# Query and key rows kept in DRAM once per part and doubled by the loads

## The chip, the cores and the metric

One core of a Trainium2 chip runs one transformer block. The metric is the device time of one launch in microseconds; the core has a matrix engine (TensorE, PE below; PEld is its weight load), VectorE (DVE), ScalarE (ACT), GpSimd (POOL) and SyncE (SP), and here SP issues every DMA.

## The reference

What is computed, cut to what matters (batch 1, S = 2048 rows, D = 512, 32 heads of 16):

```python
mod = (silu(c) @ w_mod).reshape(1, 6, 1, D)         # sa, ca, ga, sb, cb, gb
h = layernorm(x) * (1 + ca) + sa
q, k, v = split(h @ wqkv)                           # each [32, S, 16]
p = softmax(q @ k.T * 16 ** -0.5)
x = x + ga * ((p @ v).reshape(S, D) @ wo)
h = layernorm(x) * (1 + cb) + sb
x = x + gb * (mish(h @ w1 + b1) @ w2)               # w1: [512, 1792]
```

## The kernel before, in words

**Products of two parts.** A float32 value is kept as two parts, hi (rounded to the format in which PE multiplies) and lo (the rest). A product of two such values is taken as hi·hi + hi·lo + lo·hi. For a score of one head this is one matmul over 64 rows of a Q tile and a K tile: 3 x 16 = 48 rows hold the three combinations, row 48 and 49 of the Q tile hold the negated running maximum in two parts (mt) against rows of ones in K, and the other rows are zeros. Two heads share a tile, one at partitions 0 to 63 and one at 64 to 127 (`s` in the code).

**Where the rows lie.** A projection unit (`qk_unit`, one of Q or K, one of four column blocks `ct` of 8 heads, one of four blocks `tb` of 512 sequence rows) leaves a bank of 128 x 512 in PSUM. Its `fin` makes qh and ql of it, and `put` stores them to DRAM: to `qscr` for Q (50 rows for each head: hi, hi, lo of the first of the 16 values, hi, hi, lo of the second, and so on, then two rows of zeros) and to `kscr` for K (48 rows: hi, lo, hi of each value). For Q these are three DMAs, qh being stored twice; for K two, one of them with qh twice. A pair of heads `pp` is brought back by `load_q` (one DMA for each head, 50 x 512 values) and `load_k` (one for each head, 48 x 2048) into tiles `qa` and `ka`, of which there are five each, used in turn.

**The stages.** In the prologue (up to about 52 us) the layer norm, the first Q and K projections and part of V are made; for each `tb` the K block of the first 8 heads is stored and then loaded into the tiles of the first two pairs (`load_k(pp, tb)`, 48 x 512 for each head), while `load_q(pp, 48)` loads their Q. After this `constants` writes zeros, and copies of ones (line L1318) fill the K tiles 2 to 4. Then come steps `t`, two half steps `h` each. From t = -20 on a step makes maximum tiles (L471 on PE, reduced on DVE at L473) and the projections that are left (L126), from t = 0 on also scores (L507, with the exponential on ACT at L515), the product with V (L535) and, between them, the remaining projections and the MLP of earlier rows (L132). Sixteen steps are a group of four heads (two pairs) and 512 Q rows; there are 32 groups.

**What sets the order.** The program is written in the order in which each engine is to work. Work for SP hangs on half steps (`at(h, ...)`): the maximum rows of group n go out at half step 32n - 5 (`put` in `max_rows`, L496, four small DMAs into rows 48 and 49 of the `qa` tiles), the group's second pair is loaded five half steps after the rows of the group before, and the first pair earlier. SP takes its DMAs strictly in order: one that waits holds back all behind it. The DMAs share eight completion semaphores in turn, so a DMA also waits for the one issued eight before it. In the kernel's tail no Q or K load is left.

**Tiles with few buffers.** qh and ql have two buffers each, so the third unit's copies wait until the first unit's stores have landed. The weights of the next projection (`slice_load`, wr, L214) have one buffer; ACT and POOL split them into wh and wl (L91, L98) before the next units run. Projections use two banks in turn.

Of the kernel before, what the change touches and what calls it, by code (L numbers as in the profile page):

```python
# [8 lines left out]
F32 = mybir.dt.float32  # L9
# [9 lines left out]
def adaln_block(ctx: ExitStack, tc: tile.TileContext, x, wqkv, wo, w1, b1, w2, c, w_mod, out):  # L19
    nc = tc.nc  # L20
    P = 128
    S, D = x.shape[1], x.shape[2]
    F = w1.shape[1]
    H = 32
    DH = D // H
    DK = D // P
    FT = F // P
    TB = 512
# [23 lines left out]
    dram = ctx.enter_context(tc.tile_pool(name="dram", bufs=1, space=DRAM))  # L52
    ps = ctx.enter_context(tc.tile_pool(name="ps", bufs=1, space=PSUM))

    kscr = dram.tile([H, 48, S], F32, name="kscr")
    qscr = dram.tile([H, 50, S], F32, name="qscr")
    vscr = dram.tile([G, P, VROW], F32, name="vscr")
    woscr = dram.tile([DK, P, 2, D], F32, name="woscr")
    w1scr = dram.tile([FT, P, 2, D], F32, name="w1scr")
# [26 lines left out]
    def dap(t, off, ap):  # L86
        return bass.AP(tensor=t.tensor, offset=t.offset + off, ap=ap)

    def hi_copy(eng, hi, src):
        if eng == "a":  # L90
            nc.scalar.copy(hi, src)  # L91
        elif eng == "v":
            nc.vector.tensor_copy(hi, src)
        else:
            nc.gpsimd.tensor_scalar(hi, src, 1.0, 0.0, op0=ALU.mult, op1=ALU.add)

    def lo_sub(eng, lo, src, hi):
        (nc.gpsimd if eng == "p" else nc.vector).tensor_sub(lo, src, hi.bitcast(F32))  # L98
# [12 lines left out]
    def mm3(acc, ah, al, bh, bl, late="a"):  # L111

        n = len(ah)
        seq = ((ah, bh), (ah, bl), (al, bh)) if late == "a" else ((ah, bh), (al, bh), (ah, bl))
        seq = [(l[k], r[k]) for l, r in seq for k in range(n)]
        for i, (l, r) in enumerate(seq):
            mm(acc, l, r, i == 0, i == len(seq) - 1)
# [20 lines left out]
    def pe_run():  # L138
        while pe_queue:
            mm_go(pe_queue.pop(0))  # L140
# [13 lines left out]
    def bank(tag="ms"):  # L154
        return ring() if tag == "ring" else ps.tile([P, TB], F32, tag=tag, name="bk", bufs=1)
# [25 lines left out]
    def clear(h):  # L181

        return h if h < 60 or h % 32 < 25 else h - h % 32 + 34

    def at(h, f):

        hooks.setdefault(h, []).append(f)
# [29 lines left out]
    def slice_split(kind, i, pool=None, eng="p"):  # L217
        raw = slices[kind, i]
        w = raw.shape[2]
        hi = (pool or qp).tile([P, DK, w], F32R, tag="wh", name="wh", bufs=2)  # L220
        lo = (pool or qp).tile([P, DK, w], F32R, tag="wl", name="wl", bufs=2)
        hi_copy("a", hi, raw)
        lo_sub(eng, lo, raw, hi)
        slices[kind, i] = (hi, lo)

    def qk_unit(kind, ct, tb, tag):

        wh, wl = slices[kind, ct]
        acc = bank(tag)
        ts_ = slice(tb * TB, (tb + 1) * TB)  # L230
        mm3(acc, [wh[:, k, :] for k in range(DK)], [wl[:, k, :] for k in range(DK)],
            [h_h[:, k, ts_] for k in range(DK)], [h_l[:, k, ts_] for k in range(DK)], "b")

        def fin(h=None):
            qh = qp.tile([P, TB], F32R, tag="qh", name="qh", bufs=2)
            ql = qp.tile([P, TB], F32R, tag="ql", name="ql", bufs=2)
            if h is None:
                hi_copy("a", qh, acc)
                lo_sub("v", ql, acc, qh)
            else:  # L240
                qf = ql.bitcast(F32)
                nc.scalar.copy(qf, acc)
                hi_copy("p", qh, qf)
                lo_sub("p", ql, qf, qh)
            scr, rows = (qscr, 50) if kind == 0 else (kscr, 48)

            def put():
                put_away.add((kind, ct, tb))
                o = 8 * ct * rows * S + tb * TB
                if kind == 0:  # L250
                    for r, src in ((2, ql), (0, qh), (1, qh)) if h else ((0, qh), (1, qh), (2, ql)):
                        nc.sync.dma_start(dap(scr, o + r * S, [[rows * S, 8], [3 * S, DH], [1, TB]]), src.bitcast(F32))
                    return
                hi = qh.bitcast(F32)
                twice = bass.AP(tensor=hi.tensor, offset=hi.offset, ap=[list(hi.ap)[0], [0, 2], [1, TB]])
                both = (dap(scr, o, [[3 * S, P], [2 * S, 2], [1, TB]]), twice),                     (dap(scr, o + S, [[3 * S, P], [1, TB]]), ql.bitcast(F32))
                for to, src in reversed(both) if h else both:
                    nc.sync.dma_start(to, src)

            put() if h is None else at(clear(h + (5 if h > 60 else 2)), put)  # L260
        return fin
# [22 lines left out]
                put() if h is None else at(h + 1, put)  # L284
        return fin

    def load_q(pp, rows=50):
        n, j = divmod(pp, 2)
        qb, g = divmod(n, G)
        h = 4 * g + 2 * j  # L290
        qt = qa[pp % NR].bitcast(F32)
        assert (0, h // 8, qb) in put_away, (pp, put_away)
        for s in range(2):
            nc.sync.dma_start(qt[64 * s:64 * s + rows, :], qscr[h + s, :rows, qb * TB:(qb + 1) * TB])

    def load_k(pp, tb=None):
        n, j = divmod(pp, 2)
        h = 4 * (n % G) + 2 * j
        kt = ka[pp % NR].bitcast(F32)
        at_ = slice(0, S) if tb is None else slice(tb * TB, (tb + 1) * TB)  # L300
        assert {(1, h // 8, i) for i in (range(NB) if tb is None else (tb,))} <= put_away, (pp, put_away)
        for s in range(2):
            nc.sync.dma_start(kt[64 * s:64 * s + 48, at_], kscr[h + s, :, at_])

    def load_pair(pp):
        load_q(pp)
        load_k(pp)


    with ExitStack() as es:  # L310
# [23 lines left out]
        zer = lp.tile([P, TB], F32, name="zer")  # L334
# [12 lines left out]
        def stats_tb(tb):  # L347

            mv = lp.tile([P, 4, 2], F32, tag="ln_mv4", name="ln_mv4", bufs=2)
            rs = rss[tb] = lp.tile([P, 4, 4], F32, tag="ln_rs4", name="ln_rs4", bufs=3)  # L350
            for i in range(4):
                st_ = lp.tile([P, 6], F32, tag="ln_st", name="ln_st", bufs=4)
                nc.vector.bn_stats(out=st_, in_=xts[4 * tb + i])
                nc.vector.bn_aggr(out=mv[:, i, :], in_=st_)
            nc.gpsimd.tensor_scalar(rs[:, 0, :], mv[:, :, 1], 1.0, EPS, op0=ALU.mult, op1=ALU.add)
            nc.gpsimd.tensor_scalar(rs[:, 3, :], mv[:, :, 0], -1.0, 0.0, op0=ALU.mult, op1=ALU.add)
            nc.gpsimd.tensor_tensor(rs[:, 1, :], rs[:, 0, :], nhalf.to_broadcast([P, 4]), op=ALU.pow)
            nc.gpsimd.tensor_mul(rs[:, 2, :], rs[:, 3, :], rs[:, 1, :])
# [38 lines left out]
        def zeros(i):  # L397
            for b in (48, 112):
                nc.sync.dma_start(qa[i][b:b + 16, :].bitcast(F32), zer[:16, :])
# [6 lines left out]
        def constants():  # L406
            for i in range(2, NR):
                zeros(i)
            for q4 in range(S // TB):
                nc.sync.dma_start(dap(qscr, 48 * S + q4 * TB, [[50 * S, H], [S, 2], [1, TB]]), zer[:64, :])  # L410
            nc.sync.dma_start(dap(vscr, VROW - 16, [[VROW, P], [P * VROW, G], [1, 16]]), zer[:, :16 * G])
            nc.sync.dma_start(b1c, b1.rearrange("(f p) -> p f", p=P))

        def unit(fin):
            pe_run()
            fin()

        for tb in range(NB):
            if tb + 2 < NB:
                stats_tb(tb + 2)  # L420
            if tb == 0:
                slice_split(2, 0, eng="v")
            parts = []
            for kind in (1, 0) if tb == 0 else (1,):
                fin = qk_unit(kind, 0, tb, "ring")
                parts.append((pe_queue[2 * DK:], fin))
                del pe_queue[2 * DK:]
                pe_run()
            if tb in (1, 2):
                for kc in (2 * tb - 2, 2 * tb - 1):  # L430
                    unit(v_unit(0, kc, "ring"))
            if tb + 1 < NB:
                tr_tb(tb + 1, CUT1)
            for late, fin in parts:
                pe_queue.extend(late)
                unit(fin)
            if tb + 1 < NB:
                tr_tb(tb + 1, CUT2)
            if tb + 2 < NB:
                apply_tb(tb + 2)  # L440
            if tb == 0:
                for pp in range(2):
                    load_q(pp, 48)
            for pp in range(2):
                load_k(pp, tb)
        constants()
        slice_split(1, 1)

# [3 lines left out]
    ap = ctx.enter_context(tc.tile_pool(name="ap", bufs=1, reuse_waits="tile"))  # L452
# [909 lines left out]
```

## Time and profile before

| | us |
|---|---|
| median of three runs | 1707.33 (1706.47 to 1710.11) |
| the profiled execution's own time | 1705.91 |
| its span, first to last instruction | 1704.1 |
| PE busy in the span | 1667.8 |
| DVE busy | 1427.7 |
| ACT busy | 1342.4 |
| mean share of the 16 DMA engines, q1 | 48.9% |
| HBM written | 51.44 MB |

PE works in all but about 36 us of the span. In the rows below, a timeline row has start, length, engine, line, operation, out<-in and, in brackets, how long the engine stood idle before it and what ended that; SPq is the issue of a DMA, and its length is the time on the queue, not the transfer's. A row of the waits has the sum, the number and the longest of the waits. A row of windows has the stretch, its length, then the busy time of PE, PEld, DVE, ACT and POOL with instruction counts, the granted PE clock, the DMA share and GB/s. A row of a tile's view has shortest, median and longest duration in ns.

### The profile page before, as it was taken

The numbers are of one execution on the slowest core, as the hardware profiler recorded it, in microseconds if no ns is written. First come the engines' busy times: TensorE is split into PE (matmuls) and PEld (weight loads), VectorE is DVE, ScalarE is ACT, GpSimd is POOL, SyncE is SP. The second block draws the span as 40 slices with busy tenths as digits, with TensorE's granted clock in tenths as the row PEclk, the third lists the DMA queues.
The fourth block names the chain that finished last, engine by engine and source line by source line (L and its number), as shares of the span: only waits on it lengthen the run. The fifth ranks groups of instructions, "written<-read, shape, count | busy, mean of one in ns | idle before, by whom it ended". The sixth has DMA issues, their size and how long they took to land.

```text
span 1704.1 us, 32797 instructions
## 1 busy us (share of the span) xinstructions
PE 1667.8 (98%) x12236; PEld 929.6 (55%) x12236; DVE 1427.7 (84%) x2352; ACT 1342.4 (79%) x2605; POOL 889.5 (52%) x868
## 2 busy tenths in 40 slices
PE   7999999999999999999999999999999999999998
PEld 5755665555435455555555555555555555554677
DVE  6888898888898888888888888888888888881467
ACT  6247777777778898888889898888888888889364
POOL 5155215565503288755524397654534597646642
PEclk9999999999999999999999999999999999999999
DMA  7677567776772342435343644334442635332362
GB/s 242 186 223 214 128 160 211 245 233 212 237 207 58 109 128 73 126 80 148 90 127 74 189 109 96 101 108 125 114 102 73 174 99 130 93 106 82 124 225 72
DMA packets 113992, 240.03 MB, mean 141 GB/s; under 512 B 24048, under 2 KB 49648, under 8 KB 107784
## 3 DMA queue, kind: packets, MB, share of 16 engines
q1 hardware_dynamic: 113832, 237.92, 48.9%
q8 instruction: 97, 1.59, 0.4%
q14 instruction: 63, 0.52, 0.1%
HBM read 179.95 MB, written 51.44 MB: 136 GB/s over the span
## 4 chain that ended last, share of the span: by engine, by line
PE 85%; POOL 6%; ACT 3%; DMA 3%; DVE 1%; issue 1%; SPq 1%; DVEq 0%; ACTq 0%; POOLq 0%
PE bk L535 27%; PE ring L471 22%; PE ring L507 20%; PE bk L132 8%; PE bk L126 3%; PE ring L126 2%; ACT pr L515 2%; PE ring L1062 1%; DMA qa<-mt 1%; DMA wr<-in_A_wqkv 1%; POOL y L881 1%; DMA wm<-in_w_mod 1%; POOL rr L767 1%; POOL ee L765 1%; POOL hb L768 1%
## 5 line engine op out<-in xcount | busy, mean ns | idle before, releaser
L473 DVE TENSOR_REDUCE mx<-ring 128x1 f32<-128x512 f32 x2048 | 1277.1, 684 | 171.0 <-PE bk L132 111.7
L515 ACT ACTIVATE pr<-ring 128x512 f32<-128x512 f32 x2048 | 1090.6, 607 | 228.2 <-PE bk L132 163.6
L471 PE MATMUL ring<-ka,qa 64*128 64x512 f32 x2048 | 778.6, 426 | 2.2 <-ACT pr L515 1.8
L507 PE MATMUL ring<-qa,ka 64*128 64x512 f32 x2048 | 720.1, 396 | 10.3 <-DMA qa<-mt 4.8
L471 PEld LDWEIGHTS ring<-ka,qa 64*128 64x128 f32 x2048 | 365.9, 184 | 411.8 <-DVE mx L473 355.3
L535 PE MATMUL bk<-pr,vg 128*32 128x512 f32 x4096 | 545.2, 605 | 0.0
L507 PEld LDWEIGHTS ring<-qa,ka 64*128 64x128 f32 x2048 | 374.3, 185 | 118.9 <-ACT pr L515 38.5
L132 PE MATMUL bk<-h,w 64*128 64x512 f32 x1008 | 281.3, 410 | 0.0
L132 PE MATMUL bk<-w,a_h 64*128 64x512 f32 x576 | 194.4, 417 | 0.6 <-ACT pr L515 0.4
L132 PEld LDWEIGHTS bk<-h,w 64*128 64x128 f32 x1008 | 172.1, 184 | 4.9 <-ACT pr L515 0.2
L535 PEld LDWEIGHTS bk<-pr,vg 128*32 128x32 f32 x4096 | 80.9, 108 | 126.6 <-issue 119.6
L735 POOL TENSOR_SCALAR ee<-hb 128x512 f32<-128x512 f32 x42 | 62.5, 1488 | 100.2 <-ACT hb L729 91.8
L132 PE MATMUL bk<-w,a_l 64*128 64x512 f32 x288 | 113.5, 394 | 0.0
L765 POOL TENSOR_TENSOR ee<-ee,rr 128x512 f32<-128x512 f32 x42 | 54.0, 1285 | 110.7 <-ACT rr L756 110.5
L132 PEld LDWEIGHTS bk<-w,a_h 64*128 64x128 f32 x576 | 95.3, 185 | 5.9 <-ACT pr L515 1.6
L881 POOL TENSOR_TENSOR y<-yd,y 128x512 f32<-128x512 f32 x50 | 64.3, 1287 | 44.5 <-ACT yd L880 44.5
L132 PE MATMUL bk<-w,o_hl 64*128 64x512 f32 x288 | 79.7, 409 | 0.0
L98 POOL TENSOR_TENSOR a_l<-hb,a_h 128x512 fp32r<-128x512 f32 x53 | 71.7, 1352 | 4.4
L749 POOL TENSOR_SCALAR rr<-ee 128x512 f32<-128x512 f32 x42 | 26.1, 622 | 59.8 <-ACT ee L741 59.7
L132 PE MATMUL bk<-h_h,wl 64*128 64x512 f32 x168 | 57.2, 421 | 0.0
L769 POOL TENSOR_TENSOR hb<-hb,rr 128x512 f32<-128x512 f32 x42 | 54.5, 1298 | 3.3
L750 POOL TENSOR_TENSOR ee<-ee,rr 128x512 f32<-128x512 f32 x42 | 54.1, 1288 | 3.5
(204 smaller groups left out, 1822.4 us busy)
## 6 DMA issues: line engine op xcount, KB each, us to landing
ka<-kscr SPq DMA_DIRECT2D x124, 384.0 KB
w<-w2scr SPq DMA_DIRECT2D x56, 512.0 KB
w<-w1scr SPq DMA_DIRECT2D x46, 512.0 KB
vg<-vscr SPq DMA_DIRECT2D x32, 552.0 KB
qa<-qscr SPq DMA_DIRECT2D x124, 100.0 KB
kscr<-qh SPq DMA_DIRECT2D x16, 512.0 KB
qscr<-qh SPq DMA_DIRECT2D x32, 256.0 KB
hl<-in_B_w SPq DMA_DIRECT2D x28, 256.0 KB
```

Source lines behind the costliest of these rows:

```text
L98: (nc.gpsimd if eng == "p" else nc.vector).tensor_sub(lo, src, hi.bitcast(F32))
L126: nc.tensor.matmul(acc, l, r, start=start, stop=stop)
L132: i = nc.tensor.matmul(acc, l[64 * g:64 * g + 64], r[64 * g:64 * g + 64], start=start, stop=stop)
L471: nc.tensor.matmul(pm, qt[64 * s:64 * s + 64, qs * P:(qs + 1) * P], kt[64 * s:64 * s + 64, kb * TB:(kb + 1) * TB], start=True, stop=True)
L473: return nc.vector.tensor_reduce(out=mxs[n][:, s, 4 * j + qs, kb:kb + 1], in_=pm, op=ALU.max, axis=AX.X)
L507: nc.tensor.matmul(p_, kt[64 * s:64 * s + 64, kc * P:(kc + 1) * P], qt[64 * s:64 * s + 64, :], start=True, stop=True)
L515: e = nc.scalar.activation(pr, p_, AF.Exp, scale=SCALE)
L535: nc.tensor.matmul(accs[n][32 * h:32 * h + 32, :], vgs[n][:, o:o + 32], pts.pop((t, h)), start=(kc == 0), stop=(kc == 15))
L735: nc.gpsimd.tensor_scalar_min(buf("ee", 2), b["hb"], HCAP)
L765: nc.gpsimd.tensor_mul(ee, ee, rr)
L769: nc.gpsimd.tensor_mul(hb, hb, rr)
L881: nc.gpsimd.tensor_add(y[i], yd, y[i])
```

## The change

Each part is stored once. `qscr` has for each head 16 rows of hi, then 16 of lo, then the two of zeros; `kscr` 16 rows of lo, then 16 of hi. So Q and K units have two stores each, both written by head. `load_q` reads rows 0 to 33 to partitions 16 to 49 and rows 0 to 15 again to partitions 0 to 15, giving hi, hi, lo, zeros; `load_k` reads 32 rows and then the 16 of hi again, giving lo, hi, hi. The tiles have the same 48 rows for PE, in blocks of 16 and not interleaved; no PE, DVE, ACT or POOL instruction is changed or moved. The code is four lines shorter ahead of the loads, so L252 stands for both kinds of store, and the loads are L289 and L299, the maximum rows L492.

```diff
-    kscr = dram.tile([H, 48, S], F32, name="kscr")
-    qscr = dram.tile([H, 50, S], F32, name="qscr")
+    kscr = dram.tile([H, 2 * DH, S], F32, name="kscr")
+    qscr = dram.tile([H, 2 * DH + 2, S], F32, name="qscr")
...
-            scr, rows = (qscr, 50) if kind == 0 else (kscr, 48)
+            scr, rows, first = (qscr, 2 * DH + 2, 0) if kind == 0 else (kscr, 2 * DH, DH)
...
-                if kind == 0:
-                    for r, src in ((2, ql), (0, qh), (1, qh)) if h else ((0, qh), (1, qh), (2, ql)):
-                        nc.sync.dma_start(dap(scr, o + r * S, [[rows * S, 8], [3 * S, DH], [1, TB]]), src.bitcast(F32))
-                    return
-                hi = qh.bitcast(F32)
-                twice = bass.AP(tensor=hi.tensor, offset=hi.offset, ap=[list(hi.ap)[0], [0, 2], [1, TB]])
-                both = (dap(scr, o, [[3 * S, P], [2 * S, 2], [1, TB]]), twice),                     (dap(scr, o + S, [[3 * S, P], [1, TB]]), ql.bitcast(F32))
-                for to, src in reversed(both) if h else both:
-                    nc.sync.dma_start(to, src)
+                both = [(first, qh), (DH - first, ql)]
+                for r, src in both[::-1] if h else both:
+                    nc.sync.dma_start(dap(scr, o + r * S, [[rows * S, 8], [S, DH], [1, TB]]), src.bitcast(F32))
...
-    def load_q(pp, rows=50):
+    def load_q(pp, zeros=2):
...
-            nc.sync.dma_start(qt[64 * s:64 * s + rows, :], qscr[h + s, :rows, qb * TB:(qb + 1) * TB])
+            for to, n_ in ((DH, 2 * DH + zeros), (0, DH)):
+                nc.sync.dma_start(qt[64 * s + to:64 * s + to + n_, :], qscr[h + s, :n_, qb * TB:(qb + 1) * TB])
...
-            nc.sync.dma_start(kt[64 * s:64 * s + 48, at_], kscr[h + s, :, at_])
+            for to, of, n_ in ((0, 0, 2 * DH), (2 * DH, DH, DH)):
+                nc.sync.dma_start(kt[64 * s + to:64 * s + to + n_, at_], kscr[h + s, of:of + n_, at_])
...
-                nc.sync.dma_start(dap(qscr, 48 * S + q4 * TB, [[50 * S, H], [S, 2], [1, TB]]), zer[:64, :])
+                nc.sync.dma_start(dap(qscr, 2 * DH * S + q4 * TB, [[(2 * DH + 2) * S, H], [S, 2], [1, TB]]), zer[:64, :])
...
-                    load_q(pp, 48)
+                    load_q(pp, 0)
```

Three places of SP's order show what it moves. The first is the prologue, the stores of the first K and Q block and the Q load of the first pair, before:

```order
L258 DMA kscr<-qh 128x2x512
L258 DMA kscr<-ql 128x512
L252 DMA qscr<-qh 8x16x512 x2
L252 DMA qscr<-ql 8x16x512
L294 DMA qa_106<-qscr 48x512 x2
```

and now:

```order
L252 DMA kscr<-qh 8x16x512
L252 DMA kscr<-ql 8x16x512
L252 DMA qscr<-qh 8x16x512
L252 DMA qscr<-ql 8x16x512
L289 DMA qa_106<-qscr 32x512
L289 DMA qa_106<-qscr 16x512
```

One of three Q stores is gone, the K stores have the shape of the Q stores, and each head's load is two (the rows shown are those of one head; the second head's follow).

The second is the next K block in the prologue, its stores between the loads of two blocks, before:

```order
L303 DMA ka_105<-kscr 48x512 x2
L258 DMA kscr<-qh 128x2x512
L258 DMA kscr<-ql 128x512
L303 DMA ka_104<-kscr 48x512 x2
L303 DMA ka_105<-kscr 48x512 x2
```

and now (ka_104 and ka_105 are the tiles of the first two pairs):

```order
L299 DMA ka_105<-kscr 16x512
L252 DMA kscr<-qh 8x16x512
L252 DMA kscr<-ql 8x16x512
L299 DMA ka_104<-kscr 32x512
L299 DMA ka_104<-kscr 16x512
```

Between the stores of two blocks stand eight loads where four stood.

The third is one of the places between half steps 112 and 256 at which a Q unit's stores stand ahead of the maximum rows, before:

```order
L655 DMA woscr<-hl 128x1024
L458 DMA vg<-vscr 128x1104
L252 DMA qscr<-ql 8x16x512
L252 DMA qscr<-qh 8x16x512 x2
L648 DMA hl<-in_A_wo 128x512
L655 DMA woscr<-hl 128x1024
L496 DMA qa_106<-mt 2x4x128 x2
```

and now:

```order
L651 DMA woscr<-hl 128x1024
L454 DMA vg<-vscr 128x1104
L252 DMA qscr<-ql 8x16x512
L252 DMA qscr<-qh 8x16x512
L644 DMA hl<-in_A_wo 128x512
L651 DMA woscr<-hl 128x1024
L492 DMA qa_106<-mt 2x4x128 x2
```

One DMA of 256 KB less stands ahead of the maximum rows; the pair's loads, eight now, follow behind them as before.

## The prediction

> **What bounds the kernel now.** I read the page's busy times first, then the list of what TensorE (PE) waited for, then the SyncE (SP) queue's timeline, because every DMA of this kernel is issued there and the change only edits DMAs.
>
> ```profile
> span 1704.1 us, 32797 instructions
> PE 1667.8 (98%) x12236; PEld 929.6 (55%) x12236; DVE 1427.7 (84%) x2352; ACT 1342.4 (79%) x2605; POOL 889.5 (52%) x868
> ...
> PE ring L383 <- DMA wma<-in_w_mod: 10.9, 2, 10.3
> PE ring L507 <- DMA qa<-mt: 4.8, 4, 2.6
> ...
> PE ring L126 <- POOL wm L620: 0.7, 1, 0.7
> ```
>
> The reader is to see that PE sets the end: only 1704.1 - 1667.8 = 36.3 us of the span are without a matmul. No row says that PE waits for a Q or K load, so nothing can be won there. What DMAs cost PE after the start is 4.8 us for the two maximum rows (mt) and 0.7 us behind the modulation weights. So the change can win some 5 us, and it can lose wherever later DMAs make PE wait. I therefore followed SP through the first 110 us.
>
> ```profile
> 39.33 1.79 SPq L294 DMA_DIRECT2D qa<-qscr  x4
> 41.16 1.82 SPq L303 DMA_DIRECT2D ka<-kscr  x4
> 43.07 0.38 SPq L258 DMA_DIRECT2D kscr<-qh  x1
> 43.55 0.41 SPq L258 DMA_DIRECT2D kscr<-ql  x1
> 47.08 1.71 SPq L303 DMA_DIRECT2D ka<-kscr  x4
> ...
> 54.27 1.85 SPq L303 DMA_DIRECT2D ka<-kscr  x4
> ...
> 59.97 1.99 SPq L303 DMA_DIRECT2D ka<-kscr  x4
> ...
> 72.78 3.88 SPq L1318 DMA_DIRECT2D ka<-ka  x6
> 76.71 0.64 SPq L214 DMA_DIRECT2D wr<-in_A_wqkv  x1
> ```
>
> SP is here a chain without a hole of its own: it stores a block of K, waits until the store has landed (43.96 to 47.08), issues the loads, stores the next block, and then works through zeros, ones and the next weights. The load of those weights (wr) is the link to the other engines:
>
> ```profile
> 81.02 0.62 ACT L91 CAST wh<-wr 128x512 fp32r<-128x512 f32 x1 [2.53 <-DMA wr<-in_A_wqkv]
> 82.54 0.59 ACT L242 COPY ql<-bk 128x512 f32<-128x512 f32 x1 [0.90 <-PE bk L126]
> 85.97 0.85 PE L126 MATMUL bk<-h_h,wh 128*128 128x512 f32 x3
> 95.46 0.63 POOL L95 TENSOR_SCALAR qh<-ql 128x512 fp32r<-128x512 f32 x1 [6.63 <-DMA kscr<-qh]
> 100.68 0.38 SPq L214 DMA_DIRECT2D wr<-in_A_wqkv  x1
> 102.19 2.96 SPq L496 DMA_DIRECT2D qa<-mt  x4
> 105.74 0.47 PE L507 MATMUL ring<-qa,ka 64*128 64x512 f32 x1 [0.79 <-DVE mx L473]
> ```
>
> ScalarE (ACT) already stood 2.53 us for wr. The next thing it does is to empty the bank of the first K unit (82.54 to 83.13), and PE needs that bank again at 85.97: 2.8 us of slack. GpSimd (POOL) stood 6.63 us until a K store had landed, and the maximum rows left SP at 102.19, after all of this in SP's order; PE waited 0.79 us before the first score matmul at 105.74. (That row names DVE, which had long been going; the scores need the mt rows issued just before.) So at mt the slack is nothing.
>
> **The change, part by part.** No PE, DVE, ACT or POOL instruction is added or moved; the arithmetic is the same with its 48 rows in another order. Only DMAs change.
>
> *Loads split in two.* Every Q load and every K load of a head becomes two. In the piece above these are 4 more Q issues and 4 x 4 more K issues. The rows give 1.79 / 4 = 0.45 and 1.82 / 4 = 0.46 us for one: 20 x 0.455 = 9.1 us on the chain. Bounds: no row of these loads is under 0.29 us (below), 5.8 us; the 16-row copies of L1318 take 3.88 / 6 = 0.65 us, 13 us.
>
> *One Q store less.* Ahead of 39.33 stood three stores of Q; now two. That saves one issue, and its time in the queue.
>
> ```profile
> L294 SPq DMA_DIRECT2D qa<-qscr x128: 285/323/1257, 39.3 to 1503.2; - x128
> L252 SPq DMA_DIRECT2D qscr<-ql x16: 572/638/992, 33.7 to 457.5; - x16
> L258 SPq DMA_DIRECT2D kscr<-ql x16: 326/422/1197, 31.8 to 301.8; - x16
> q1 hardware_dynamic: 113832, 237.92, 48.9%
> ```
>
> The issue is 0.64 us. In the queue: 48.9% of 16 engines over 1704.1 us is 13333 us of engine time for 113832 packets, 0.117 us for one of 2.1 KB on average. 128 rows of 2 KB are 15.0 us of engine time, 0.94 us if 16 engines share it, 1.9 us if the eight heads that are now outermost go to eight; I take 1.3 us. Together -1.9 us.
>
> *K stores in the form of the Q stores.* Two of 256 KB instead of one of 512 KB and one of 256 KB, but written by head like Q: 0.638 - 0.422 = 0.22 us more for each issue, 8 issues, +1.7 us. The data are a third less (-0.9 us each time if spread as now) or on half the engines (+0.9 us); I take 0.
>
> Sum on the way to wr: 9.1 - 1.9 + 1.7 = +8.9 us. Less 2.8 us of slack this stops PE at 85.97 for some 6 us. Then the next pair's four more issues (1.8 us) come ahead of the K stores for which POOL stood at 95.46, so the shift at mt is 8.9 + 1.8 = 10.7 us, less what holes of SP take up; I take **+10.5 us**, from 7 to 15. It is not added to the 6 us: PE loses the larger. Were this chain covered by other PE work, the term would be zero, but PE has only maximum tiles and projections here, and both come behind the same stopped bank.
>
> *The third Q store, later.* Where mt is late afterwards, a Q unit's stores stand ahead of it on SP:
>
> ```profile
> 427.48 1.84 SPq L252 DMA_DIRECT2D qscr<-qh  x2
> ...
> 432.68 3.48 SPq L496 DMA_DIRECT2D qa<-mt  x4
> ...
> 341.00:343.00 2.00, 0.84 (x8) 0.50 (x8) 0.69 (x1) 0.29 (x2) 1.84 (x2) 1.00 0.46 130
> 388.00:390.00 2.00, 1.11 (x10) 0.51 (x7) 1.01 (x2) 0.62 (x2) 1.90 (x2) 1.00 0.54 154
> 435.00:438.60 3.60, 1.00 (x12) 0.22 (x4) 1.34 (x3) 0.95 (x2) 1.54 (x2) 0.96 0.69 217
> 438.60:441.80 3.20, 3.20 (x16) 2.00 (x20) 1.35 (x3) 1.95 (x4) 3.03 (x5) 0.51 0.98 214
> ```
>
> In the windows PE stands 1.16, 0.89 and 2.60 us; after the longest the granted clock is 0.51 for 3.2 us, 1.6 us more. A store less takes 1.3 us out of the queue ahead of mt: the first two stalls go, the third keeps 1.3 us and, being then no longer than stalls that left the clock at 1.00, should not lower it: 1.16 + 0.89 + 1.3 + 1.6 = **-5.0 us**. Bounds: -6.3 (all of it) and 0.
>
> *Two tight loads.* From the second group on each pair has four more issues, 1.9 us. SP mostly idles (it stands 193.7 us for DVE at L496 alone), so what follows on SP is covered, and the loads themselves end well ahead of use, except at two places:
>
> ```profile
> SPq L496 <- DVE mx L473: 193.7, 18, 15.7
> ...
> 108.33 9.19 DMA wm<-in_w_mod
> ...
> 131.18 0.78 SPq L303 DMA_DIRECT2D ka<-kscr  x2
> ...
> 141.55 0.49 PE L471 MATMUL ring<-ka,qa 64*128 64x512 f32 x1
> ...
> 483.40 0.80 SPq L303 DMA_DIRECT2D ka<-kscr  x2
> ...
> 495.12 0.49 PE L471 MATMUL ring<-ka,qa 64*128 64x512 f32 x1
> ```
>
> Pair 4 has 9.6 us from its last issue to its first maximum tile, behind weight loads that take up to 9.19 us to land; pair 19 has 10.9 us behind four weight loads, and the sums of the finished group come right after it. I take all of the 1.9 us at each, **+3.8 us** (0 to 7). The modulation weights come 1.9 us sooner against the rest: **-0.7 us**.
>
> **Sum.** 10.5 - 5.0 + 3.8 - 0.7 = +8.6 us: span 1712.7 us, the profiled execution 1705.91 + 8.6 = 1714.5 us, and with the 1.4 us by which the median lies above it **1716 us**. Ends: 7 - 6.3 - 0.7 = 0 and 15 + 7 = +22 us.
>
> **The rivals.**
>
> *Faster: the chain is covered.* If a piece of 16 or 32 rows issues in half the time of one of 48, the first 80 us stay as they are, wr lands inside its 2.8 us of slack, and only the lighter Q stores count: -5.7 us, 1701.6 us. It decides for an issue under about 0.3 us. For it speaks that 0.29 occurs; against it, that in the first 60 us four issues take 1.7 to 2.0 us in every row, whatever stands ahead. Chance 0.06.
>
> *No change.* The chain grows by about 5 us (the lower bound of the issues) and the Q stores give it back: 1707 us. Chance 0.09.
>
> *Much slower: the uneven piece.* The later Q piece has 34 rows, which do not divide among 16 engines. On two engines each carries 17 rows, 17 x 0.117 = 2.0 us, twice for a pair, 4.0 us against 1.2 us for 50 rows on ten: +2.8 us in front of the K rows on those engines. If that and the 1.9 us of issues exceed the slack of every second pair (those that wait for the group before to end, some 30) by 1 to 2 us, it costs 30 to 60 us on top of the rest: about 1761 us. Against it: between those loads and their use lie over 11 us, as from 483.40 to 495.12. Chance 0.07. The Trainium skill has the rule, on the page "DMA: Bandwidth & Descriptors", section "Why a DMA increments its semaphore by 16 and not by 1": a DMA runs on the largest number of engines up to 16 that divides the outermost sizes of both sides. By that rule 34 rows run on 2 engines, 50 on 10, 48 on 16, and a store by eight heads on 8. No row quoted here shows the number of engines.
>
> **How the numbers follow.** My forecast has 0.78, the rivals 0.06, 0.09 and 0.07. A measurement of this kernel tells about 0.2% (3.4 us) from no change. The forecast's own range is 1709 to 1728 us; taking in the no-change case, 1706 to 1728 us. A little of the forecast lies under 1710.7: faster 0.06, same 0.11, slower 0.83.
>
> **What would show it.** In the changed profile: SP reaches the copies ka<-ka some 9 us later than 72.78; ACT waits about 11 us for wr instead of 2.53; PE has a stall of several us near 86 and the first score matmul is near 116 instead of 105.74; the mt waits of 1.16 and 0.89 us are gone and the third is halved with the clock at 1.00. I am wrong in the main term if L1318 starts within 4 us of 72.78, or if PE does not stand before 110 us; and wrong on the steady part if PE's list of waits shows Q or K loads from 550 us on.

## The result, and the profile after

| | before | changed |
|---|---|---|
| median, us | 1708.66 (1706.47 to 1710.11, 4 runs) | 1755.82 (1752.78 to 1758.29, 4 runs) |
| profiled execution, us | 1705.91 | 1755.88 |
| ratio to before, 95% interval | | 1.0276 (1.0255 to 1.0297) |

The change costs 47 us. The direction was forecast; the size was not, and the range ended at 1728.

First the changed kernel's span, its busy times and the list of what PE waited for (total us, times, longest):

```profile
span 1754.1 us, 33140 instructions
PE 1686.8 (96%) x12236; PEld 939.3 (54%) x12236; DVE 1428.7 (81%) x2352; ACT 1342.9 (77%) x2605; POOL 889.1 (51%) x868
...
PE bk L126 <- ACT ql L242: 14.6, 3, 7.8
PE ring L379 <- DMA wma<-in_w_mod: 10.5, 2, 10.0
PE ring L503 <- DMA qa<-mt: 8.6, 4, 3.4
PE ring L467 <- DMA ka<-kscr: 5.5, 2, 3.8
```

Two things stand there. PE is idle for 1754.1 - 1686.8 = 67.3 us instead of 36.3, and the same 12236 matmuls take 1686.8 us instead of 1667.8, 19 us more. Most of that is a lower clock: in the trace's clock records PE has half of its clock for 45.8 us of the span instead of 3.4. It works in 35.6 us of these instead of 3.2, and half of the difference is 16 us. The new waits are for ql (ACT cannot empty the projection's bank) and for the K load of a pair; there is also more waiting for mt, though a Q store in front of mt was removed.

The SP queue's timeline, for the places that the prediction followed:

```profile
51.84 4.43 SPq L299 DMA_DIRECT2D ka<-kscr  x8
...
63.70 3.65 SPq L299 DMA_DIRECT2D ka<-kscr  x8
...
72.94 3.56 SPq L299 DMA_DIRECT2D ka<-kscr  x8
...
85.64 3.83 SPq L1314 DMA_DIRECT2D ka<-ka  x6
89.51 0.68 SPq L214 DMA_DIRECT2D wr<-in_A_wqkv  x1
...
102.93 0.65 SPq L252 DMA_DIRECT2D kscr<-ql  x1
...
121.03 3.00 SPq L492 DMA_DIRECT2D qa<-mt  x4
```

The copies ka<-ka start 12.9 us later than in the kernel before (85.64 against 72.78), the maximum rows 18.8 us later (121.03 against 102.19). ACT and PE follow (rows of their timelines, idle time and releaser in brackets):

```profile
93.90 0.62 ACT L91 CAST wh<-wr 128x512 fp32r<-128x512 f32 x1 [14.34 <-DMA wr<-in_A_wqkv]
109.84 0.59 ACT L242 COPY ql<-bk 128x512 f32<-128x512 f32 x1 [14.35 <-DMA kscr<-ql]
...
95.06 1.65 PE L126 MATMUL bk<-h_h,wh 128*128 128x512 f32 x3 [7.85 <-ACT ql L242]
110.48 1.30 PE L126 MATMUL bk<-h_h,wh 128*128 128x512 f32 x3 [4.51 <-ACT ql L242]
124.01 1.63 PE L126 MATMUL bk<-h_h,wh 128*128 128x512 f32 x4 [2.23 <-ACT ql L242]
128.43 0.76 PE L503 MATMUL ring<-qa,ka 64*128 64x512 f32 x1 [2.79 <-DMA qa<-mt]
```

ACT waits twice, once for wr and once for a K store that has to free ql. PE stands four times, 17.4 us together, and the first score matmul starts at 128.43 instead of 105.74. Later it stands for a K load and for mt, which windows of the trace show (length; busy us of PE, PEld, DVE, ACT, POOL; granted clock, as a share of the full one; DMA share; GB/s):

```profile
95.00:106.00 11.00, 10.91 (x36) 6.62 (x36) 6.55 (x11) 0.49 (x2) 4.61 (x5) 0.74 0.91 210
...
163.00:173.00 10.00, 6.18 (x39) 2.87 (x33) 4.58 (x10) 3.30 (x8) 4.38 (x5) 0.83 0.55 175
...
374.00:385.00 11.00, 7.62 (x44) 3.91 (x36) 4.41 (x8) 4.37 (x9) 6.84 (x7) 0.69 0.57 135
```

In these three windows, which hold or follow a stall, the granted clock is 0.74, 0.83 and 0.69. Not every stall has that: from 335 to 345 us PE stands for 2.2 us and the clock stays at 1.00.

The next table places the loss in time, here and for the experiments below. It gives, for some pairs, how much later their first maximum matmul starts than in the kernel before (us; worked out from the matmul records of the profiled executions, where these starts are 94.9, 116.7, 166.2, 329.2, 451.1, 589.5 and 1515.7).

| kernel | pair 2 | 3 | 5 | 12 | 17 | 23 | 63 |
|---|---|---|---|---|---|---|---|
| changed | +16.8 | +23.1 | +27.4 | +33.7 | +36.6 | +44.6 | +50.4 |
| e1_split | +8.0 | +8.0 | +9.3 | +9.5 | +15.9 | +18.4 | +19.7 |
| e3_mirror | +11.4 | +15.3 | +19.1 | +24.4 | +17.7 | +17.8 | +19.2 |
| e5_kspread | +5.7 | +5.4 | +4.5 | +4.7 | -1.1 | -0.1 | +1.6 |
| e7_wr | +14.5 | +17.8 | +22.0 | +23.5 | +17.3 | +17.4 | +18.6 |
| e8_cut34 | +12.5 | +15.0 | +21.4 | +24.9 | +40.5 | +52.7 | +62.6 |
| e9_khead | +14.5 | +16.2 | +20.4 | +20.8 | +14.4 | +17.5 | +19.0 |
| e6_48 | -0.6 | -1.4 | -2.3 | -2.3 | -9.4 | -9.2 | -7.8 |

For the changed kernel 44.6 of the 50.4 us are lost before pair 23. The stretch from pair 23 to pair 63, more than half of the span, loses almost nothing; of the last 5.8 us, 4.3 fall between pairs 35 and 36 and pairs 51 and 52.

### The profile page after: what moved, and what is told of

It is laid out like the page before. It is cut to its first block, busy times and chain, and to the rows that moved or that the text cites. A ratio compares the mean times of both kernels' runs of the same rounds, so it can differ in the third digit from the quotient of the medians.

```text
span 1754.1 us, 33140 instructions
## 1 busy us (share of the span) xinstructions
PE 1686.8 (96%) x12236; PEld 939.3 (54%) x12236; DVE 1428.7 (81%) x2352; ACT 1342.9 (77%) x2605; POOL 889.1 (51%) x868
## 4 chain that ended last, share of the span: by engine, by line
PE 73%; POOL 10%; DMA 8%; ACT 3%; SPq 2%; DVE 2%; issue 1%; POOLq 0%; ACTq 0%; DVEq 0%
PE bk L531 23%; PE ring L467 18%; PE ring L503 17%; PE bk L132 8%; PE ring L126 3%; DMA qa<-qscr 2%; DMA ka<-kscr 2%; PE bk L126 2%; ACT pr L511 1%; PE ring L1058 1%; POOL rr L763 1%; POOL ee L761 1%; POOL hb L764 1%; DMA sm<-ot 1%; POOL ee L731 1%
## 5 line engine op out<-in xcount | busy, mean ns | idle before, releaser
L467 PE MATMUL ring<-ka,qa 64*128 64x512 f32 x2048 | 788.1, 431 | 11.2 <-DMA ka<-kscr 5.5
L761 POOL TENSOR_TENSOR ee<-ee,rr 128x512 f32<-128x512 f32 x42 | 53.9, 1283 | 106.7 <-ACT rr L752 106.5
L98 POOL TENSOR_TENSOR wl<-wr,wh 128x512 fp32r<-128x512 f32 (+1 forms) x13 | 17.7, 1362 | 75.4 <-ACT wh L91 75.4
```

The source lines that it names most:

```text
L467: nc.tensor.matmul(pm, qt[64 * s:64 * s + 64, qs * P:(qs + 1) * P], kt[64 * s:64 * s + 64, kb * TB:(kb + 1) * TB], start=True, stop=True)
L761: nc.gpsimd.tensor_mul(ee, ee, rr)
```

## The experiments

Three theories stood at the start. **I**: the 20 more load issues hold SP up, and the rest follows (the prediction's main term). **U**: the load of 34 rows goes through few DMA engines and holds up what comes behind it (the prediction's last rival, but wherever it acts). **S**: K's stores by head land too late.

**e1_split: only the loads split.**

```diff
-nc.sync.dma_start(qt[64 * s:64 * s + rows, :], qscr[h + s, :rows, ...])
+for a, b in ((0, 32), (32, rows)):
+    nc.sync.dma_start(qt[64 * s + a:64 * s + b, :], qscr[h + s, a:b, ...])
```

(and K's load likewise, at 32 and 48).

> The kernel before with only its loads split (rows 0 to 31, then 32 to 49 of Q or 32 to 47 of K); stores and layout as before. Theory I (the added load issues hold SP up in the prologue, and ScalarE, TensorE and the maximum rows behind it): the copies ka<-ka some 9 us later than 72.78, most of the loss is here, 1735 to 1750 us. Theory U (the 34-row piece is what costs): no piece here has 34 rows, so under 1722 us. Theory S (K's stores by head land later): under 1725 us.

Measured 1726.49 us, ratio 1.0111 (1.0083 to 1.0138). Splitting costs 19 us, less than half of the loss and outside what any of the three had said; by the table half of it comes before pair 5 and half between pairs 12 and 23. In the first half SP's copies start at 80.23 us, 7.5 later than in the kernel before, the maximum rows leave at 109.82, 7.6 later, and PE's longest stall at the bank is 5.3 us. In the second half PE waits for mt (6.8 us between 320 and 600 us) and once for a K load (1.8 us).

**e2_kstore: K's stores by head.**

```diff
-both = (dap(scr, o, [[3 * S, P], [2 * S, 2], [1, TB]]), twice), ...
+both = (dap(scr, o, [[rows * S, 8], [3 * S, DH], [2 * S, 2], [1, TB]]), twice), ...
```

> The kernel before with only K's stores written by head (8 outermost, the upper half still twice in one DMA); loads as before. Theory I: each of four waits for a store grows by about 1 us, 3 to 4 us at ka<-ka, about what ScalarE's bank has in hand: 1708 to 1716 us. Theory S: 1725 us and more. Theory U: 1708 us.

Measured 1707.26 us, ratio 0.9992 (0.9978 to 1.0005), but this does not say that the form costs nothing: with 48 rows to a head the two strides are one (48 = 3 x 16), and in the trace these stores have the 16 semaphore updates of the kernel before, where stores by head have 9. So the edit changed nothing; e9_khead tests the form with other row counts.

**e3_mirror: the halves mirrored, so that Q is cut into 32 and 18 rows.**

```diff
-scr, rows, first = (qscr, 2 * DH + 2, 0) if kind == 0 else (kscr, 2 * DH, DH)
+scr, rows, first = (qscr, 2 * DH + 2, DH) if kind == 0 else (kscr, 2 * DH, 0)
...
-for to, n_ in ((DH, 2 * DH + zeros), (0, DH)):
+for to, of, n_ in ((0, 0, 2 * DH), (2 * DH, DH, DH + zeros)):
...
-for to, of, n_ in ((0, 0, 2 * DH), (2 * DH, DH, DH)):
+for to, of, n_ in ((DH, 0, 2 * DH), (0, 0, DH)):
```

> The changed kernel with the two parts of Q and of K mirrored (Q's lower half first, K's upper half first), so that Q's pieces have 32 and 18 rows instead of 34 and 16; as many DMAs and bytes. Theory U (34 rows on two engines): most of the loss goes, under 1730 us. Theory I or S: 1748 to 1757 us, since nothing on SP changes.

Measured 1723.48 us, ratio 1.0086 (1.0059 to 1.0113). As many DMAs, issues and bytes as the changed kernel, and 1755.82 - 1723.48 = 32.3 us are gone. Theory U holds for the larger part of the loss. PE's waits behind these DMAs are now three at the bank, one for K and one for mt:

```profile
PE bk L126 <- ACT ql L242: 13.0, 3, 9.6
...
PE ring L467 <- DMA ka<-kscr: 3.2, 1, 3.2
...
PE ring L503 <- DMA qa<-mt: 2.0, 1, 2.0
```

The table places the gain: 8.3 us up to pair 5 (27.4 - 19.1), 18.5 more up to pair 23 (44.6 - 17.8 = 26.8), 4.4 more by pair 63.

**e4_qwhole: the changed kernel with Q stored three times and loaded whole.**

```diff
-both = [(first, qh), (DH - first, ql)]
+both = [(first, qh), (DH - first, ql)] if kind else [(0, qh), (DH, qh), (2 * DH, ql)]
-for to, n_ in ((DH, 2 * DH + zeros), (0, DH)):
-    nc.sync.dma_start(qt[64 * s + to:64 * s + to + n_, :], qscr[h + s, :n_, ...])
+n_ = 3 * DH + zeros
+nc.sync.dma_start(qt[64 * s:64 * s + n_, :], qscr[h + s, :n_, ...])
```

> The changed kernel with Q as before in number: stored three times by head, loaded by one DMA of 50 rows per head; K as changed. Theory I: 8 of the 24 more load issues up to the third pair's go, one Q store of about 0.6 us and its time come back: ka<-ka about 3 us earlier than 85.64 and about a third of the loss goes, 1735 to 1745 us. Theory U: under 1725 us. Theory S: 1745 us and more.

Measured 1735.63 us, ratio 1.0161 (1.0129 to 1.0192). In theory I's range, but not for its reason: e3_mirror has eight more Q issues in the prologue and for pairs 2 and 3, and is 12 us faster. What e4 has beside it is a third Q store and loads of 50 rows; which of the two costs the 12 us was not tested.

**e8_cut34 and e11_cut31: the number of rows in a piece alone.** e1_split with Q cut at 34 (the diff), then with 31 in its place.

```diff
-for a, b in ((0, 32), (32, rows)):
+cut = 34 if rows == 50 else 32
+for a, b in ((0, cut), (cut, rows)):
```

> As e1_split (the kernel before with split loads), but Q cut into 34 and 16 rows instead of 32 and 18: as many DMAs, bytes and issues. Theory U (a piece of 34 rows goes through few engines and holds up what follows it): 15 to 30 us above e1_split, 1740 to 1757 us. Rival (what e3_mirror gained lay in the order of the halves or in the stores): 1724 to 1730 us.

> As e8_cut34, cut at 31 (pieces of 31 and 19 rows). If a load runs on the largest divisor of its rows up to 16, both pieces go through one engine: more than e8_cut34, 1790 us and above. If 34 costs because it is over 32, or because any cut off a multiple of 16 does: 1725 to 1770 us.

Measured 1767.35 us, ratio 1.0349 (1.0325 to 1.0374), and 1917.42 us, ratio 1.1244 (1.1185 to 1.1303). Moving the cut from 32 to 34 costs 41 us and to 31 (with 19 behind) costs 191 us, in a kernel whose layout and stores are those of before; so it is not that 34 is more than 32. What the pieces do is seen in the trace's semaphore updates (a DMA adds to its semaphore as its parts land) and in the time from issue to the last update, the landing. A pair's loads go out head by head, so each head has its own column:

| DMA, kernel | rows | semaphore updates of one DMA | first head, us | second head, us |
|---|---|---|---|---|
| Q load, e3_mirror | 32 / the 18 behind | 16 / 10 | 2.06 / 1.88 | 2.08 / 2.45 |
| Q load, before | 50 | 11 | 2.92 | 3.69 |
| Q load, changed | 34 / the 16 behind | 3 / 16 | 4.16 / 3.93 | 6.51 / 6.34 |
| Q load, e11_cut31 | 31 / the 19 behind | 2 / 2 | 5.75 / 9.00 | 11.33 / 12.32 |
| K load behind, e3_mirror | 32 | 16 | 4.14 | 5.55 |
| K load behind, changed | 32 | 16 | 6.99 | 7.78 |
| K load behind, e11_cut31 | 32 | 16 | 12.60 | 12.39 |

(Medians over the pairs loaded in one go between 300 and 560 us, worked out from the issue records and semaphore updates.) The first head's load of 34 rows lands 2.1 us later than one of 32, the second head's, which goes out behind it, 4.4 us later. The 16 rows behind land with them, and the K loads are 2 to 3 us later though they are unchanged. By the Trainium skill ("DMA: Bandwidth & Descriptors", "Why a DMA increments its semaphore by 16 and not by 1") k engines, the largest number up to 16 that divides the outermost sizes of both sides (here the rows), each add one, after one step for the rest: 34 rows run on 2, 50 on 10, 18 on 9, 31 and 19 on 1. The updates agree: k + 1 wherever k is under 16. The same section says that these are the lowest-numbered engines, which would put the mt rows (3 updates) on the same two; no run here shows which engines they were. That the loads follow one another through the same few engines fits the landings, in which each Q load of 2 or 3 updates takes longer than the one before it.

What PE waits for in e11_cut31 shows where it ends once the piece is slow enough:

```profile
PE ring L474 <- DMA ka<-kscr: 39.9, 17, 8.5
PE ring L474 <- DMA od<-ot: 27.8, 12, 3.0
PE ring L510 <- DMA qa<-mt: 23.6, 7, 7.8
```

Now K loads are late in 17 places, and the steady part loses too: pair 23 is 132.2 us late and pair 63 is 205.9. At 34 rows the steady part loses little (52.7 and 62.6 us for e8_cut34). The landings fit this: between a K load's issue and its use lie some 11 to 12 us (483.40 and 495.12 in the rows of the prediction), more than the 7.8 us at 34 rows and less than the 12.4 us at 31.

**e5_kspread: K's stores over 128 partitions again.** e3_mirror with hi and lo of a part alternating in DRAM, so that one stride runs over all 128 rows.

```diff
-nc.sync.dma_start(dap(scr, o + r * S, [[rows * S, 8], [S, DH], [1, TB]]), ...)
+nc.sync.dma_start(dap(scr, o + r * S,
+                      [[rows * S, 8], [2 * S, DH], [1, TB]] if kind == 0 else [[2 * S, P], [1, TB]]), ...)
```

(and the 16- and 18-row loads take every second row).

> As e3_mirror, but hi and lo rows of a part alternate, so that K's stores run over 128 partitions in one stride instead of 8 heads by 16; as many DMAs and bytes, the loads cut into 32 and 16 or 18 rows as there. Theory I2 (behind the split loads there is no slack left, and then a K store that lands 2 to 3 us later counts each time): pair 5 some 10 us after its time in the kernel before instead of 19, 1711 to 1717 us. Rival (the form of the stores costs nothing, as e2_kstore had it): 1721 to 1725 us.

Measured 1706.33 us, ratio 0.9997 (0.9986 to 1.0009): the whole of the loss that e3_mirror still had, 17 us, and more than expected. SP in this kernel:

```profile
45.91 0.38 SPq L252 DMA_DIRECT2D kscr<-ql  x1
48.24 3.56 SPq L300 DMA_DIRECT2D ka<-kscr  x8
...
78.28 3.82 SPq L1316 DMA_DIRECT2D ka<-ka  x6
...
91.14 0.93 SPq L252 DMA_DIRECT2D kscr<-ql  x1
...
106.45 2.87 SPq L494 DMA_DIRECT2D qa<-mt  x4
```

All the added load issues are still there, yet the copies start only 5.5 us later than in the kernel before, and PE's longest stall here is small:

```profile
PE bk L126 <- ACT ql L242: 4.4, 2, 2.9
```

**e9_khead: the same with 8 heads outermost.** e5_kspread with two unused rows behind each head's K rows; nothing else differs.

```diff
-kscr = dram.tile([H, 2 * DH, S], F32, name="kscr")
+kscr = dram.tile([H, 2 * DH + 2, S], F32, name="kscr")
-... [[rows * S, 8], [2 * S, DH], [1, TB]] if kind == 0 else [[2 * S, P], [1, TB]] ...
+... [[rows * S, 8], [2 * S, DH], [1, TB]] ...
```

> As e5_kspread, with two unused rows behind each head's K rows, so that K's stores can't run over 128 partitions in one stride and go by 8 heads again; hi and lo still alternate, the pieces and bytes are the same. (The edit of e2_kstore had left both strides equal, 48 rows to a head being 3 times 16, and so wrote the same DMAs as before.) Theory I2 (a store with 8 outermost goes through half of the engines and lands later): 1718 to 1728 us, as e3_mirror. Rival (what e5_kspread gained lay in the order of the rows in DRAM): 1704 to 1710 us.

Measured 1724.95 us, ratio 1.0101 (1.0073 to 1.0129): 18.6 us for the store's outermost size. That it is not the padding itself is seen in e3_mirror, which stores K by head without it and takes 1723.48 us. Its rows beside those of e5_kspread:

```profile
47.53 0.58 SPq L252 DMA_DIRECT2D kscr<-ql  x1
52.31 4.43 SPq L300 DMA_DIRECT2D ka<-kscr  x8
...
86.10 3.83 SPq L1316 DMA_DIRECT2D ka<-ka  x6
...
99.02 0.91 SPq L252 DMA_DIRECT2D kscr<-ql  x1
...
95.54 1.65 PE L126 MATMUL bk<-h_h,wh 128*128 128x512 f32 x3 [9.41 <-ACT ql L242]
```

From the end of a K store's issue to the loads that wait for it, SP stands 52.31 - 48.11 = 4.2 us instead of 48.24 - 46.29 = 1.95. In the next two blocks it stands 5.4 and 4.2 us instead of 4.6 and 2.05, so 5.2 us more in all, and the copies are 7.8 us later. The store of qh (9 semaphore updates instead of 16) takes 6.78 us to land instead of 4.94 (medians from 40 to 130 us), and mt, behind it, 3.86 instead of 1.81.

**e7_wr: is wr the link?** e3_mirror with the load of wr ahead of zeros, ones and copies.

```diff
-at(-2 * PRO, lambda: slice_load(*plan[2][1:3]))
...
+slice_load(0, 1)
 constants()
```

> As e3_mirror, with the load of the next weights (wr) issued ahead of the zeros, ones and copies, about 11 us sooner. Theory I (the issues delay wr, and ScalarE and TensorE with it): ScalarE's wait of 16.06 us for wr shrinks to under 5, TensorE's stall of 9.56 us to under 4, 1714 to 1719 us. Rival (the K stores behind it hold the chain whatever wr does): 1721 to 1725 us.

Measured 1724.69 us, ratio 1.0104 (1.0074 to 1.0135): no gain. The wait for wr went as expected, but the stall did not:

```profile
80.72 0.62 ACT L91 CAST wh<-wr 128x512 fp32r<-128x512 f32 x1 [2.16 <-DMA wr<-in_A_wqkv]
...
107.13 0.58 ACT L242 COPY ql<-bk 128x512 f32<-128x512 f32 x1 [20.29 <-DMA kscr<-ql]
...
107.76 1.65 PE L126 MATMUL bk<-h_h,wh 128*128 128x512 f32 x3 [13.43 <-ACT ql L242]
...
96.47 1.78 SPq L299 DMA_DIRECT2D ka<-kscr  x4
...
99.37 0.65 SPq L252 DMA_DIRECT2D kscr<-ql  x1
```

ACT copies two units early, and then the third waits 20.29 us for the first one's K store, which stands in SP's order behind the copies and pair 2's loads (issued at 99.37 us, against 96.62 in e3_mirror). SP's lateness sets the end through that store as well; taking one of the two links away gives nothing.

**e6_48, e12_q48 and e10_even: even loads and stores.** Here the maximum product runs over 48 rows instead of 64, so Q's two zero rows, and the four DMAs that write them, are not needed.

```diff
-nc.tensor.matmul(pm, qt[64 * s:64 * s + 64, ...], kt[64 * s:64 * s + 64, ...], ...)
+nc.tensor.matmul(pm, qt[64 * s:64 * s + 48, ...], kt[64 * s:64 * s + 48, ...], ...)
```

e12_q48 is the kernel before with this and Q loads of 48 rows. e6_48 has in addition 48 rows to a head in qscr, and Q stored as K is: `[[3 * S, P], [S, 2], [1, TB]]` for qh and `[[3 * S, P], [1, TB]]` for ql. e10_even is e5_kspread with the 48 rows and Q's stores over 128 partitions.

> The kernel before, with the maximum product taken over 48 rows instead of 64, so that Q needs no two zero rows: Q loads of 48 rows instead of 50, no zero stores, and Q stored in K's form (the upper half twice in one DMA, over 128 partitions). If Q's uneven loads and its third store by head cost time in the kernel before too: the waits for mt (4.8 us and the low clock after) go, 1698 to 1704 us. If they are hidden: 1706 to 1709 us.

> As e5_kspread, with the maximum product over 48 rows, so that Q has no zero rows (pieces of 32 and 16, no zero stores), and Q stored over 128 partitions as K is. All of the change's DMAs are then even. If even loads are what matters: about e6_48's gain, 1696 to 1702 us. If the more issues of split loads cost beside that: 1702 to 1708 us.

> The kernel before with the maximum product over 48 rows, Q loads of 48 rows instead of 50 and no zero stores; Q is still stored three times, by head (8 outermost), as before. It parts e6_48's gain of 9 us. If the third store by head holds mt up: mt waits stay, 1704 to 1709 us. If the uneven loads of 50 rows (and the zero stores) do: the mt waits go, 1697 to 1702 us.

| kernel | us | ratio to before, 95% |
|---|---|---|
| e12_q48 | 1707.32 | 1.0011 (0.9997 to 1.0025) |
| e6_48 | 1698.31 | 0.9951 (0.993 to 0.9971) |
| e10_even | 1702.16 | 0.9967 (0.9954 to 0.998) |

Loads of 48 instead of 50 rows give nothing by themselves: in e12_q48 the mt wait stays, and with it the low clock behind it (window 435 to 441 us). In e6_48 the list has no wait for mt, and the same window is whole:

```profile
PE ring L505 <- DMA qa<-mt: 3.4, 3, 1.6
...
435.00:441.00 6.00, 4.95 (x27) 2.17 (x29) 2.46 (x5) 2.28 (x5) 5.75 (x7) 0.72 0.91 174
```

```profile
435.00:441.00 6.00, 6.00 (x50) 3.21 (x52) 5.29 (x9) 5.03 (x10) 3.01 (x3) 1.00 0.98 326
```

So the gain comes from Q's stores, two over 128 partitions instead of three by head. e6_48 is 9 us faster than the kernel before; e10_even, which moves less data with more loads, came out 4 us above it, with intervals that overlap. It lies on the border between its two expected ranges, so it leaves open whether the added issues still cost something.

## Why the prediction was wrong

The forecast was +8.6 us; +47 were measured. The runs make a ladder: before 1707.7; loads split, 1726.5 (e1_split); Q and K stored once per part, with K's stores over 128 partitions and no load of 34 rows, 1706.3 (e5_kspread); K's stores by head, 1725.0 (e9_khead); and with the 34-row piece the changed kernel, 1755.8, for which e3_mirror (1723.5) is the kernel without that piece. What the change is about comes out even (19 us for the split loads, 20 back from the stores and the data); 19 us and 32 us are owed to how the two DMAs happened to be cut. The steps hold in this order only: the same 34 rows cost 41 us from e1_split to e8_cut34.

- **"K stores in the form of the Q stores ... I take 0"** is the step of the sum that failed first. The effect was seen ("on half the engines (+0.9 us)") and set against the lighter data. Measured, e5_kspread to e9_khead: 18.6 us. The 0.9 us was engine time; what counts is that SP waits for the landing in each block (5.2 us more in three), that ACT waits for it later (19.7 us for K stores in all, instead of 11.8), and that PE then stands at the bank (12.5 us instead of 4.4).
- **The uneven piece** is the larger one, 32 us, which the sum left out. Kind and size were right: 2.0 us for a piece, 4.0 for a pair and 2.8 in front of K were priced; measured are 2.1, 4.4 and 2.2 to 2.9. What failed is the place: "some 30" steady pairs, against which the 11 us of slack were held up, so that it was given 0.07. That slack does hold at 34 rows: no K wait shows from 550 us on, and the sign that was to prove the steady part wrong did not come; e11_cut31 shows what happens when it does not hold. But the piece also stands ahead of K's loads, K's stores and mt from pair 2 on and up to 560 us, where little has slack, and there it costs 27 of the 31 us by which the two profiled executions differ. That the rival's 1761 us came out near the 1755.8 measured is luck: it was worked out for a place where nearly nothing is lost.
- **The prologue chain, +10.5 us.** Where the issues stand alone it holds nearly: in e1_split the copies are 7.5 us late instead of 9.1, PE's stall is 5.3 us where some 6 were forecast, and pair 5 is 9.3 us late. In e5_kspread, with the same issues and without the two uneven forms, it is less, 5.5 us at the copies and 4.5 at pair 5; in the first block SP waits 1.95 us there for the smaller spread stores, where the kernel before stood 3.1. In the changed kernel the copies are 12.9 us late and pair 5 is 27.4. The signs forecast were there (ACT's wait for wr, the stall near 86, a late first score matmul), only larger: 14.34 against 11, 7.85 against several, 128.43 against 116. That wr is the link was half true: e7_wr shows that K's store behind the same SP work is one as well.
- **The third Q store, -5.0 us.** Right in size where it can be seen alone: e5_kspread gains 4.7 + 1.1 = 5.8 us between pairs 12 and 17, and e12_q48 against e6_48 shows that Q's stores, not its loads, are what mt stands behind. In the changed kernel the piece of 34 rows took the gain back (+2.9 us between the same pairs).
- **Two tight loads, +3.8 us.** The stall at pair 4 is there (the 3.8 us of the waits' row), and the shift grows from 40.0 to 44.5 us between pairs 19 and 20; but for the larger part it is the 34 rows and the late stores ahead of the loads, not their issues: e1_split, with the issues alone, loses 1.3 us at pair 4 and 1.4 at pair 20, and in e5_kspread, with the same issues, it is -1.0 and +0.9 us.

## What to carry to other kernels

Before cutting or padding a DMA, write down the outermost sizes of both its sides, and look in a trace how many semaphore updates it makes: a store of 8 by 16 rows instead of 128 (9 updates instead of 16) cost as much here as all the added loads, 19 us, and a piece of 34 rows instead of 32 (3 updates instead of 16) cost 32 to 41 us. A slow DMA is not priced by its own consumer: list what stands behind it on the same queue, and look for the phase in which those have no slack. And a shape that looks cheap in one place (two strides that happen to merge) says nothing of the same form with other row counts.

## What was not expected of the hardware

- A row of 2 KB costs on few engines about what a mean packet costs (0.117 us). With 2 rows on each engine for the load of 32, 17 for that of 34 and 31 for that of 31 (the rule cited above), the first head's landings give (4.16 - 2.06) / 15 = 0.14 us and (5.75 - 2.06) / 29 = 0.13 us for a row, an estimate. What makes these loads slow is that the rows, and the loads behind, go one after another.
- Stalls of PE can cost twice, as idle time and as a lower clock behind them. Of the 48.8 us between the spans of the changed kernel and e5_kspread, 15.9 are PE busy time (1686.8 against 1670.9 us for the same matmuls), at a granted clock as low as 0.69 and 0.74 in the windows shown.
